# Strassen's algorithm in the second MLP layer of an attention and MLP kernel

## The chip, the cores and the metric

The kernel runs on one core of one Trainium2 chip. The metric is the device time of the whole kernel in microseconds (us).

## The reference

Attention inside routing clusters, then a layer norm and an MLP with a residual, all in float32:

```python
mask = q_assign[:, :, :, None] == k_assign[:, :, None, :]
scores = np.where(mask, scale * np.matmul(q, k.transpose(0, 1, 3, 2)), -1000000000.0)
attn = np.exp(scores - np.max(scores, axis=-1, keepdims=True))
attn = attn / (np.sum(attn, axis=-1, keepdims=True) + 1e-09)
x = np.matmul(attn, v)          # then (B, H, S, D) -> (B, S, H*D)
xn = (x - mu) / np.sqrt(var + 1e-06) * g_ln
out = x + np.maximum(xn @ w_ch1, 0.0) @ w_ch2
```

Four sequences (B) of 768 tokens (S), 8 heads of 64, model width 512 (DM), hidden width 2048 (FF).

## The kernel before

**Stages.** The attention part works through 16 pairs (a sequence and two heads), in an order of PE, DVE and ACT written out by hand. Beside it the float64 weights are loaded and turned into float32 (`w1`, `w2`), and the first sequence is normed. Each pair ends in `finish`: part 0 sums the denominators (`den_ps`, which ACT copies to `dsb`, sent by DMA to `rdens`), part 1 takes the reciprocal (L380) and spreads it through DRAM to `rb`, part 2 multiplies `x` by `rb` on DVE (L394) and stores it to DRAM (`xT_d`, L395). Then `stage.close()` gives the memory of the attention's pools back, the pools of the MLP (`ps_m`, `ps_o`, `ffn`, `ffn1`) are opened over it, and the MLP runs one sequence after the other. A new pool's first tile waits for whatever was last in the memory that the whole pool covers. In the MLP only PE's order is written by hand (`manual_schedule`); a scheduler sets the order of DVE, ACT and SP, which issues the DMAs.

**First layer.** `xn` holds a normed sequence, the 512 features on the partitions (4 chunks). Its product with `w1` is made by Strassen's algorithm on 2 x 2 blocks: seven products in place of eight, for each of 8 column tiles j (`first_layer`, parts 1 to 7; PE takes them as 1, 2, 4 of the tile before, 6, 3 of the tile before, 5, 7). One product is two matmuls of 384 columns. The block sums of the weights (`ws0` to `ws3`) are made once, by `weight_sum` on DVE in pairs 8 to 11; the sums of blocks of `xn` are made by `x_sum` (L472). Partial sums stay in PSUM (`x_ps`, `z_ps`) and are taken out by ACT (`kept`) and DVE (`add_relu`). The result is 32 tiles `hidden[r, f]` of 128 x 384 (r: half of the tokens, f: chunk of 128 hidden features).

**Second layer.** `project` takes the 6 token tiles t in turn: 16 matmuls of 512 columns (`hidden` is the stationary operand, `w2` the moving one) add up in a bank `o_ps` (L644), DVE adds the rows `xb` of the residual (L654), SP stores the sum. A float32 matmul is two MATMUL instructions, each with a weight load of its own, in the trace.

**The next sequence** is normed inside the second layer: `norm_load` after t = 0, `norm_rows` (12 transposes by PE, copies by ACT into two `xr` buffers in turn, which DMAs store and whose statistics DVE takes) after t = 1 and after t = 2, `norm_stat_rows` in the middle of t = 3 (PE transposes the statistics, DMAs spread them to `stat_row`), `norm_apply` (L449, L451) and `x_sum` after t = 4.

Of the kernel before, what the change touches and what calls it, by code (L numbers as in the profile page):

```python
# [8 lines left out]
F32 = mybir.dt.float32  # L9
# [10 lines left out]
def kernel(  # L20
# [35 lines left out]
    def pool(name, bufs, **kw):  # L56
        return stage.enter_context(tc.tile_pool(name=name, bufs=bufs, **kw))
# [12 lines left out]
    def ps(name, dt=F32, n=512):  # L70
        return pools["t"].tile([P, n], dt, tag="t", name=name)
# [35 lines left out]

    onehots = []
    for side in "qk":
        oh = const.tile([P, TH, NHALF, 2, D], BF16, name=f"onehot_{side}")  # L110
        nc.gpsimd.memset(oh, 0.0)
        onehots.append(oh)

# [42 lines left out]
    def w1_block(i, l, cols):  # L156
        return w1[:, l * NDH : (l + 1) * NDH, i * FH + cols.start : i * FH + cols.stop]

    def weight_sum(i, cols):

        a, op, b = (
            (w1_block(1, 0, cols), ALU.add, w1_block(1, 1, cols)),
            (ws[0][:, :, cols], ALU.subtract, w1_block(0, 0, cols)),
            (w1_block(0, 0, cols), ALU.subtract, w1_block(1, 0, cols)),
            (w1_block(0, 1, cols), ALU.subtract, ws[1][:, :, cols]),
        )[i]
        nc.vector.tensor_tensor(ws[i][:, :, cols], a, b, op)  # L167

# [289 lines left out]
    def x_sum(b, i):

        if i == 0:  # L460
            normed[b][1:] = [
                ffn.tile([P, NDH, HC], F32, tag=f"xt{m}", name=f"xt{m}", bufs=1)
                for m in range(3)
            ]
        _, t1, t2, t4 = normed[b]
        o, a, c = (
            (t1, x_block(b, 0, 1), x_block(b, 0, 0)),
            (t2, x_block(b, 1, 1), t1),
            (x_block(b, 0, 1), x_block(b, 1, 1), x_block(b, 0, 1)),
            (t4, x_block(b, 1, 0), t2),  # L470
        )[i]
        nc.vector.tensor_tensor(o, a, c, ALU.subtract)  # L472
# [4 lines left out]
    def put(n, slot, f, *args):  # L477
        extra.setdefault((n, slot), []).append(lambda: f(*args))
# [96 lines left out]
    def product(bank, lhs, rhs, cols, first):  # L575
        for c in range(NDH):
            nc.tensor.matmul(  # L577
                bank[:, :HC], lhs[:, c, cols], rhs[:, c, :],
                start=first and c == 0, stop=c == NDH - 1,
                skip_group_check=True,  # L580
            )

    def hidden_tile(r, f):
        h = (ffn, ffn1)[r].tile([P, HC], F32, tag=f"h{r}", name=f"h{r}", bufs=NFC + 1)
        hidden[r, f] = h
        return h

    def kept(bank, tag):
        t = ffn.tile([P, HC], F32, tag=tag, name=tag)
        nc.scalar.copy(t, bank[:, :HC])  # L590
        return t

# [5 lines left out]
    sets = {}  # L598

    def first_layer(b, j, part):  # L600

        _, t1, t2, t4 = normed[b]
        cols = slice(j * P, (j + 1) * P)
        every = slice(0, FH)
        st = sets.setdefault((b, j), {})
        if part == 1:
            st["x"] = ps_m.tile([P, 512], F32, tag="x", name="x_ps")
            product(st["x"], w1_block(0, 0, every), x_block(b, 0, 0), cols, True)  # L610
            st["p1"] = kept(st["x"], "p1")
        elif part == 2:
            y = ps_m.tile([P, 512], F32, tag="y", name="y_ps", bufs=1)
            product(y, w1_block(0, 1, every), x_block(b, 1, 0), cols, True)
            add_relu(0, j, y, st["p1"])
        elif part == 6:
            product(st["x"], ws[1], t2, cols, False)
            st["u2"] = kept(st["x"], "u2")
        elif part == 5:
            st["z"] = ps_m.tile([P, 512], F32, tag="z", name="z_ps")  # L620
            product(st["z"], ws[0], t1, cols, True)
        elif part == 7:
            product(st["x"], ws[2], x_block(b, 0, 1), cols, False)
            st["u3"] = kept(st["x"], "u3")
            add_relu(1, NFH + j, st["z"], st["u3"])
        elif part == 4:
            product(st["x"], w1_block(1, 1, every), t4, cols, False)
            nc.scalar.activation(hidden_tile(0, NFH + j), st["x"][:, :HC], AF.Relu)  # L628
        elif part == 3:
            product(st["z"], ws[3], x_block(b, 1, 1), cols, False)  # L630
            add_relu(1, j, st["z"], st["u2"])

    def rows_load(b, t):
        x = ffn1.tile([P, DM], F32, tag="xb", name="xb", bufs=3)
# [4 lines left out]
    chunks = [i * NFH + j for j in range(NFH) for i in range(2)]

    def project(b, t, x, fs, op):
        r, tt = divmod(t, TH)
        for f in fs:
# [7 lines left out]
        if fs[-1] != chunks[-1]:
            return
        o = ffn1.tile([P, DM], F32, tag="o", name="o_sb", bufs=2)
        nc.vector.tensor_tensor(o, op, x, ALU.add)  # L654
        nc.sync.dma_start(out=out[b].rearrange("(p c) m -> p c m", p=P)[:, t, :], in_=o)

    with tc.manual_schedule(engines={mybir.EngineType.PE}):
        for i in range(4):
            x_sum(0, i)
        for b in range(B):  # L660
            for j in range(NFH):
                for part, ahead in ((1, 0), (2, 0), (4, 1), (6, 0), (3, 1), (5, 0), (7, 0)):
                    if j - ahead >= 0:
                        first_layer(b, j - ahead, part)
            xb = {0: rows_load(b, 0)}
            for t in range(NT):
                if t + 1 < NT:
# [12 lines left out]
                if t == 0:  # L680
                    norm_load(b + 1)
                elif t < 3:
                    for tt in range(TH):
                        norm_rows(b + 1, (t - 1) * TH + tt)
                    if t == 2:
                        norm_stats(b + 1)
                elif t == 4:
# [206 lines left out]
```

## Time and profile before

| | |
|---|---|
| three runs, us | 1034.55, 1034.86, 1035.57 (median 1034.86) |
| the profiled execution's own time, us | 1035.45 |
| its span, us | 1033.6 |
| granted TensorE clock, mean | 0.994 |
| attention, from the start to the first MLP matmul | 394 us |
| MLP | 394 us to the end: four first layers, four second layers |
| busy in the second layer of the second sequence (626 to 714 us) | PE 88.0, DVE 21.3, ACT 4.8 us |

The time is the span plus about 2 us around it. Busy PE is the union of its matmuls, whose ends are modelled; how much time a stream of matmuls takes is read from the chain of waits, which has each stretch of equal matmuls with its length and their number. The second layers are the largest piece of the chain (32% of the span), the first layers 28%.

### The profile page before, as it was taken

What the parts mean: (1) busy time and instruction counts of PE and PEld (TensorE: products, weight loads), DVE (VectorE), ACT (ScalarE), POOL (GpSimd) and SP (SyncE); (2) the same over time, 40 slices, a digit from 0 to 9 for tenths busy, and PEclk for the clock granted to TensorE, in tenths of its full rate; (3) what the DMA queues carried; (4) which work ended last, traced back from release to release, by engine and by line L of the source; (5) the groups of instructions that cost most, each with busy time, mean ns of one, the idle gap of its engine ahead of it and who ended that gap; (6) DMA issues with size and microseconds to landing.
All of it is one profiled execution on the core that took longest, in us unless ns stands there. A gap on an engine that the chain in (4) does not pass through costs nothing.

```text
span 1033.6 us, 11347 instructions
## 1 busy us (share of the span) xinstructions
PE 1011.8 (98%) x4374; PEld 498.2 (48%) x4374; DVE 508.2 (49%) x860; ACT 314.9 (30%) x516; POOL 2.8 (0%) x27
## 2 busy tenths in 40 slices
PE   6999999999999998999999999999999999999997
PEld 3444444444444444554445554444555444555443
DVE  3888888999999995321241331151222151331000
ACT  4656666667565651220101220000220000221000
POOL 1000000000000000000000000000000000000000
PEclk8999999999999999999999999999999999999999
DMA  7355555555645322002221001231000331000100
GB/s 164 87 145 143 134 138 150 142 142 137 168 126 137 100 72 92 1 0 82 76 77 41 1 1 59 73 102 41 0 1 23 110 103 41 1 1 0 41 30 23
DMA packets 104765, 77.62 MB, mean 75 GB/s; under 512 B 84176, under 2 KB 84224, under 8 KB 104704
## 3 DMA queue, kind: packets, MB, share of 16 engines
q1 hardware_dynamic: 104032, 76.79, 26.4%
q8 instruction: 36, 0.59, 0.2%
q14 instruction: 25, 0.20, 0.1%
q10 hardware_dynamic: 672, 0.03, 0.0%
HBM read 57.71 MB, written 19.00 MB: 74 GB/s over the span
## 4 chain that ended last, share of the span: by engine, by line
PE 88%; DVE 9%; issue 1%; DMA 1%; ACT 0%; SPq 0%; DVEq 0%; ACTq 0%
PE o_ps L644 32%; PE x_ps L577 16%; PE a_ps L340 9%; PE s_ps L325 9%; PE z_ps L577 8%; PE y_ps L577 4%; PE s_ps L320 3%; DVE es L354 3%; PE qk_ps L231 2%; PE x_ps L413 1%; PE sim_ps L248 1%; PE oh_ps L296 1%; PE den_ps L371 1%; DVE es L351 1%; DVE ws L167 1%
## 5 line engine op out<-in xcount | busy, mean ns | idle before, releaser
L644 PE MATMUL o_ps<-w,h 128*128 128x512 f32 x768 | 332.2, 592 | 0.0
L644 PEld LDWEIGHTS o_ps<-w,h 128*128 128x128 f32 x768 | 145.2, 190 | 178.7 <-issue 176.6
L330 ACT ACTIVATE e<-s_ps 128x768 f32<-128x768 f32 x192 | 152.3, 814 | 71.8 <-PE s_ps L325 59.6
L325 PE MATMUL s_ps<-t,t 64*128 64x384 f32 x768 | 156.4, 486 | 0.0
L340 PE MATMUL a_ps<-e,v_sb 128*64 128x384 f32 x768 | 144.8, 499 | 0.0
L595 DVE TENSOR_TENSOR h<-z_ps,u 128x384 f32<-128x384 f32 x64 | 35.7, 558 | 205.6 <-PE z_ps L577 130.3
L354 DVE TENSOR_TENSOR es<-es,e 128x768 f32<-128x768 f32 x128 | 122.2, 954 | 7.3 <-ACT e L330 0.8
L654 DVE TENSOR_TENSOR o_sb<-o_ps,xb 128x512 f32<-128x512 f32 x24 | 16.6, 691 | 186.7 <-PE o_ps L644 186.7
L340 PEld LDWEIGHTS a_ps<-e,v_sb 128*64 128x64 f32 x768 | 46.6, 136 | 86.5 <-issue 86.3
L325 PEld LDWEIGHTS s_ps<-t,t 64*128 64x128 f32 x768 | 69.2, 190 | 21.4 <-issue 21.4
L590 ACT COPY u<-x_ps 128x384 f32<-128x384 f32 x64 | 30.7, 479 | 139.7 <-PE x_ps L577 139.7
L320 PE MATMUL s_ps<-m,m 64*128 64x384 bf16 x384 | 63.9, 330 | 0.6 <-ACT e L330 0.6
L590 ACT COPY p<-x_ps 128x384 f32<-128x384 f32 x32 | 15.3, 479 | 129.8 <-PE x_ps L577 129.8
L577 PE MATMUL z_ps<-xn,ws 128*128 128x384 f32 x128 | 46.8, 488 | 2.4 <-DVE h L595 2.4
L628 ACT ACTIVATE h<-x_ps 128x384 f32<-128x384 f32 x32 | 15.7, 491 | 108.8 <-PE x_ps L577 108.8
L577 PE MATMUL z_ps<-xt,ws 128*128 128x384 f32 x128 | 47.8, 497 | 0.0
L577 PE MATMUL x_ps<-xn,ws 128*128 128x384 f32 x128 | 46.8, 488 | 0.0
L577 PE MATMUL x_ps<-xn,w 128*128 128x384 f32 x128 | 46.6, 487 | 0.0
L577 PE MATMUL x_ps<-xt,ws 128*128 128x384 f32 x128 | 46.5, 486 | 0.0
L577 PE MATMUL y_ps<-xn,w 128*128 128x384 f32 x128 | 46.5, 486 | 0.0
L577 PE MATMUL x_ps<-xt,w 128*128 128x384 f32 x128 | 46.5, 486 | 0.0
L417 ACT COPY xr<-x_ps 128x512 f32<-128x512 f32 x24 | 13.5, 588 | 101.2 <-PE x_ps L413 86.4
(101 smaller groups left out, 798.0 us busy)
## 6 DMA issues: line engine op xcount, KB each, us to landing
raw<-in_moe_w_ch_dram SPq DMA_DIRECT2D x32, 512.0 KB, 3.9
q_sb<-in_q_dram SPq DMA_DIRECT2D x32, 192.0 KB, 4.3
k_sb<-in_k_dram SPq DMA_DIRECT2D x32, 192.0 KB, 4.3
v_sb<-in_v_dram SPq DMA_DIRECT2D x32, 192.0 KB, 4.1
rb<-row SPq DMA_DIRECT2D x32, 192.0 KB, 3.4
xT_d<-x SPq DMA_DIRECT2D x16, 384.0 KB, 3.0
xn<-xT_d SPq DMA_DIRECT2D x16, 384.0 KB, 4.6
x_d<-xr SPq DMA_DIRECT2D x24, 256.0 KB, 2.8
```

Of the source, the lines that this page charges most:

```text
L231: nc.tensor.transpose(t[:, c * P : (c + 1) * P], src[:, g * TH + c, :, :].rearrange("p h d -> p (h d)"), ident,)
L320: nc.tensor.matmul(s[:, j, :HC], st["m", 1][rows[j], keys], st["m", 0][rows[j], cols], start=True, stop=False,)
L325: nc.tensor.matmul(s[:, j, :HC], st[1][rows[j], keys], st[0][rows[j], cols], start=False, stop=True,)
L330: nc.scalar.activation(e, s[:, :, :HC], AF.Exp, scale=SCALE)
L340: nc.tensor.matmul(acc[j * D : (j + 1) * D, :HC], loaded[n]["v"][:, c, j, :], e[:, j, :], start=(c == 0), stop=(c == NT - 1),)
L354: nc.vector.tensor_tensor(es, es, soft.pop(i), ALU.add)
L577: nc.tensor.matmul(bank[:, :HC], lhs[:, c, cols], rhs[:, c, :], start=first and c == 0, stop=c == NDH - 1, skip_group_check=True,)
L590: nc.scalar.copy(t, bank[:, :HC])
L595: nc.vector.tensor_tensor(h, bank[:, :HC], other, ALU.add)
L628: nc.scalar.activation(hidden_tile(0, NFH + j), st["x"][:, :HC], AF.Relu)
L644: nc.tensor.matmul(op, hidden[r, f][:, tt * P : (tt + 1) * P], w2[:, f, :], start=(f == chunks[0]), stop=(f == chunks[-1]),)
L654: nc.vector.tensor_tensor(o, op, x, ALU.add)
```

## The change

The second layer is made by Strassen's algorithm too. Its blocks are halves of the tokens (r), of the hidden features (l) and of the 512 output columns (`MH` = 256): seven products in place of eight, each of 3 token tiles tt by 8 matmuls of 256 columns (`second_layer`, parts 1 to 7). One kind of product is taken over all tt before the next, in the order 1, 2, 5, 6, 7, 4, 3. The sums of blocks of `hidden` (`hidden_sums`) are made by DVE, three of the four in place; those of `w2` (`w2_sum`) and of `w1` (`w1_sums`) are made again in every sequence, so `weight_sum` goes from the attention part. `xb` is loaded in halves of 256 columns, and the output is added and stored in such halves. `ffn1` goes: all tiles of the MLP lie in one pool `ffn`; its PSUM tiles lie in one pool of 8 banks. `norm_rows` moves behind parts 2 and 5, `norm_stat_rows` behind the first tile of part 6, `norm_apply` behind part 7, `x_sums` behind part 4. The two `onehot` tiles move to a pool that ends with the attention.

```diff
-    ws = [weights.tile([P, NDH, FH], F32, name=f"ws{i}") for i in range(4)]
...
-    for i in range(4):
-        for o in range(2):
-            put(8 + 2 * o + i // 2, (0, 3)[i % 2], weight_sum, i, slice(o * WC, (o + 1) * WC))
...
-    ps_m = pool("ps_m", 2, space=PSUM)
-    pools["t"] = pool("ps_o", 3, space=PSUM)
+    pools["t"] = pool("ps_m", 8, space=PSUM)
     ffn = pool("ffn", 2)
-    ffn1 = pool("ffn1", 1)
...
+    def w1_sums(b, j):
+        t = ffn.tile([P, 4, NDH, P], F32, tag="ws", name="ws")
...
+            nc.vector.tensor_tensor(t[:, i], x, y, op)
...
+    def w2_sum(st, i):
+        if i in (1, 3):
+            st["t", i] = ffn.tile([P, NFH, MH], F32, tag="sums", name=f"w2t{i}")
+        elif i == 2:
+            st["t", 2] = ffn.tile([P, NFH, MH], F32, tag="sums", name="w2t2")
...
+        for c in range(0, NFH, 2):
+            nc.vector.tensor_tensor(o[:, c : c + 2], x[:, c : c + 2], y[:, c : c + 2], ALU.subtract)
+
+    def hidden_sums(c, late):
+
+        a11, a12, a21, a22 = [hidden[r, l, c] for r in range(2) for l in range(2)]
+        if late:
+            nc.vector.tensor_tensor(a12, a12, a11, ALU.subtract)
+            return
+        s3 = ffn.tile([P, HC], F32, tag="hs", name="hs", bufs=NFH)
...
+        nc.vector.tensor_tensor(s3, a11, a21, ALU.subtract)
+        nc.vector.tensor_tensor(a21, a21, a22, ALU.add)
+        nc.vector.tensor_tensor(a11, a21, a11, ALU.subtract)
+
+    def second_product(bank, tt, lhs, rhs, first):
+        for c in range(NFH):
             nc.tensor.matmul(
-                op,
-                hidden[r, f][:, tt * P : (tt + 1) * P],
-                w2[:, f, :],
...
+                bank[:, :MH], hidden[lhs + (c,)][:, tt * P : (tt + 1) * P], rhs[:, c, :],
...
+    def add_rows(b, r, tt, j, bank):
+
+        x = ffn.tile([P, MH], F32, tag="xb", name="xb", bufs=4)
+        nc.sync.dma_start(out=x, in_=x_d[b][:, r * TH + tt, j * MH : (j + 1) * MH])
+        o = ffn.tile([P, MH], F32, tag="o", name="o_sb", bufs=12)
+        nc.vector.tensor_tensor(o, bank[:, :MH], x, ALU.add)
+        return o
...
+    def second_layer(b, tt, part, st):
+        if part == 1:
+            st["x", tt] = ps("x_ps")
+            second_product(st["x", tt], tt, (0, 0), w2_block(0, 0), True)
+            st["p1", tt] = add_rows(b, 0, tt, 0, st["x", tt])
+        elif part == 2:
+            y = ps("y_ps")
+            second_product(y, tt, (0, 1), w2_block(1, 0), True)
+            add_store(b, 0, tt, 0, st["p1", tt], y)
+        elif part == 5:
+            st["z", tt] = ps("z_ps")
+            second_product(st["z", tt], tt, (1, 0), st["t", 1], True)
+        elif part == 6:
+            second_product(st["x", tt], tt, (0, 0), st["t", 2], False)
+            st["u2", tt] = add_rows(b, 0, tt, 1, st["x", tt])
+        elif part == 7:
+            second_product(st["x", tt], tt, ("s3",), st["t", 3], False)
+            st["u3", tt] = add_rows(b, 1, tt, 1, st["x", tt])
+            add_store(b, 1, tt, 1, st["u3", tt], st["z", tt])
+        elif part == 4:
+            second_product(st["x", tt], tt, (1, 1), st["t", 2], False)
+            store(b, 1, tt, 0, add_rows(b, 1, tt, 0, st["x", tt]))
+        elif part == 3:
+            second_product(st["z", tt], tt, (0, 1), w2_block(1, 1), False)
+            add_store(b, 0, tt, 1, st["u2", tt], st["z", tt])
...
+            for tt in range(TH):
+                second_layer(b, tt, 1, st)
+                if tt == 0:
+                    first_layer(b, NFH - 1, 4)
+                    first_layer(b, NFH - 1, 3)
+            for c in range(NFH):
+                hidden_sums(c, False)
+            w2_sum(st, 2)
+            if more:
+                norm_load(b + 1)
+            for part in (2, 5, 6, 7, 4, 3):
+                for tt in range(TH):
+                    second_layer(b, tt, part, st)
+                    if part == 6 and tt == 0 and more:
+                        norm_stat_rows(b + 1)
+                if part == 2:
+                    for c in range(NFH):
+                        hidden_sums(c, True)
+                if part == 5:
+                    w2_sum(st, 3)
+                if part == 6:
+                    w2_sum(st, 4)
+                if more and part in (2, 5):
...
+                        norm_rows(b + 1, (0 if part == 2 else TH) + tt)
+                    if part == 5:
+                        norm_stats(b + 1)
+                if more and part == 7:
...
+                            norm_apply(b + 1, i, c)
+                if more and part == 4:
+                    x_sums(b + 1)
```

Two places of the order that the scheduler makes of it. First DVE from attention to MLP, before: `x<-x,rb` (L394) is part 2 of `finish`, L380 and L554 to L558 are part 1 for the last pair and a check that follows it, `xt` and `xn<-xn` are the sums of `xn` (L472), of which three more stand ahead of these rows, `h` the first hidden tiles.

```order
L472 TENSOR_TENSOR xt_4062<-xn,xt_4061 128x768
L595 TENSOR_TENSOR h_4075<-y_ps,p_4070 128x384
L596 TENSOR_SCALAR h_4075<-h_4075 128x384
L380 RECIPROCAL rdens<-rdens 128x12
L554 TENSOR_REDUCE ends<-rdens 128x1
L555 TENSOR_REDUCE ends<-rdens 128x1
L556 TENSOR_SCALAR ends<-ends 128x1
L557 TENSOR_SCALAR ends<-ends 128x1
L558 TENSOR_TENSOR ends<-ends 128x1
L595 TENSOR_TENSOR h_4100<-y_ps,p_4095 128x384
L596 TENSOR_SCALAR h_4100<-h_4100 128x384
L394 TENSOR_TENSOR x<-x,rb 128x768
```

And with the change (L387 is L394 of before, L373 is L380, L456 to L461 are the sums of `xn`, `ws` those of `w1`):

```order
L387 TENSOR_TENSOR x<-x,rb 128x768
L373 RECIPROCAL rdens<-rdens 128x12
L540 TENSOR_REDUCE ends<-rdens 128x1
L541 TENSOR_REDUCE ends<-rdens 128x1
L542 TENSOR_SCALAR ends<-ends 128x1
L543 TENSOR_SCALAR ends<-ends 128x1
L544 TENSOR_TENSOR ends<-ends 128x1
L387 TENSOR_TENSOR x<-x,rb 128x768
L456 TENSOR_TENSOR xt<-xn 128x768
L578 TENSOR_TENSOR ws<-w_163 128x256
L457 TENSOR_TENSOR xt<-xn,xt 128x768
L458 TENSOR_TENSOR xn<-xn 128x2x384
```

The sums of `xn` stood ahead of the last pair's reciprocal and of its L394; now they stand behind both. In the program with the change the first of them, `xt<-xn`, waits for the DMA that stores the last pair's `x` (`xT_d<-x`), because the one pool `ffn` reaches over the memory of `x` and `rb`; `ffn` of before did not, `ffn1` did.

Second, DVE behind part 5 and the second group of `norm_rows`, with the change: BN_STATS and BN_AGGR are the statistics of its three rows, `w2t` sums of `w2`, `o_sb` the first tile of part 6, L421 and L422 end the statistics that PE then transposes, L442 is `norm_apply`.

```order
L643 TENSOR_TENSOR w2t_4547<-w_164 128x512 x4
L413 BN_STATS bn<-xr 128x6 x2
L414 BN_AGGR mv<-bn 128x2 x2
L413 BN_STATS bn<-xr 128x6
L414 BN_AGGR mv<-bn 128x2
L421 COPY stat<-mv 128x6
L670 TENSOR_TENSOR o_sb<-x_ps,xb 128x256
L422 RECIPROCAL stat<-stat 128x6
L670 TENSOR_TENSOR o_sb<-x_ps,xb 128x256
L643 TENSOR_TENSOR w2t_4435<-w_164,w2t_4435 128x512 x2
L442 TENSOR_TENSOR xn<-xn,stat_row 128x768
L643 TENSOR_TENSOR w2t_4435<-w_164,w2t_4435 128x512
```

Before, no sum stood ahead of the statistics (L428 and L429 are L421 and L422 here, L449 is L442):

```order
L654 TENSOR_TENSOR o_sb<-o_ps,xb 128x512
L420 BN_STATS bn<-xr 128x6 x2
L421 BN_AGGR mv<-bn 128x2 x2
L420 BN_STATS bn<-xr 128x6
L421 BN_AGGR mv<-bn 128x2
L428 COPY stat<-mv 128x6
L429 RECIPROCAL stat<-stat 128x6
L449 TENSOR_TENSOR xn<-xn,stat_row 128x768 x2
L654 TENSOR_TENSOR o_sb<-o_ps,xb 128x512
```

The sums `w2t<-w` of four instructions, which wait for the end of part 5, now stand ahead of the second group's statistics, and the first output tile of part 6 ahead of the reciprocal.

## Rows read from the trace of the kernel before

**Rows 1.** Page, part 4: shares of the chain that ended last
```profile
PE 88%; DVE 9%; issue 1%; DMA 1%; ACT 0%; SPq 0%; DVEq 0%; ACTq 0%
```

**Rows 2.** Chain of waits in order of time: start us, us, what
```profile
464.37 2.58 PE z_ps L577 x8
...
498.29 1.44 PE x_ps L413 x12
...
955.75 70.40 PE o_ps L644 x164
...
224.28 0.67 PE oh_ps L296 x12
```

**Rows 3.** Groups by line, shapes apart: busy us, mean ns | idle before us, releaser
```profile
L644 PEld LDWEIGHTS o_ps<-w,h 128*128 128x128 f32 x768 | 145.2, 190 | 178.7 <-issue 176.6
...
L219 DVE TENSOR_TENSOR w<-tb,ta 128x512 f32<-128x512 f32 x32 | 22.1, 691 | 1.1
...
L273 DVE TENSOR_TENSOR hit<-simT_ps,best 128x384 f32<-128x384 f32 x16 | 8.9, 557 | 0.6
...
L296 PEld LDWEIGHTS <-onehot_k 128*128 128x128 bf16 x96 | 6.3, 101 | 0.0
```

**Rows 4.** Chain of waits, last matmuls on `v` of a slot, four pair ends
```profile
27.07 1.44 PE a_ps L340 x8
...
50.33 1.44 PE a_ps L340 x8
...
215.45 1.44 PE a_ps L340 x8
...
333.57 1.44 PE a_ps L340 x8
```

**Rows 5.** Groups by line: the block sums of the weights
```profile
L167 DVE TENSOR_TENSOR ws<-w 128x1024 f32<-128x1024 f32 x4 | 4.8, 1210 | 0.0
```

**Rows 6.** Timeline, attention to MLP: start us, us, engine, instruction [idle before, releaser]
```profile
394.11 0.48 ACT L376 COPY dsb<-den_ps 128x384 f32<-128x384 f32 x1 [3.53 <-PE den_ps L371]
...
404.26 0.95 DVE L394 TENSOR_TENSOR x<-x,rb 128x768 f32<-128x768 f32 x1
...
405.23 0.33 SPq L395 DMA_DIRECT2D xT_d<-x  x1
...
407.62 0.56 DVE L595 TENSOR_TENSOR h<-z_ps,u 128x384 f32<-128x384 f32 x1 [2.41 <-DMA xT_d<-x]
...
408.23 1.70 PE L577 MATMUL z_ps<-xn,ws 128*128 128x384 f32 x4 [2.37 <-DVE h L595]
```

**Rows 7.** Stretches behind that stop: us, busy us (x) of five engines, PEclk, DMA share, GB/s
```profile
409.00:410.00 1.00, 1.00 (x4) 0.63 (x3) 0.03 (x1) 0.00 (x0) 0.00 (x0) 0.76 0.87 311
...
412.00:413.00 1.00, 1.00 (x3) 0.40 (x2) 0.00 (x0) 0.00 (x0) 0.00 (x0) 0.54 0.00 0
```

**Rows 8.** The same at the kernel's start
```profile
14.00:15.00 1.00, 0.38 (x4) 0.38 (x5) 0.80 (x3) 0.00 (x0) 0.00 (x0) 0.50 1.30 212
...
19.00:20.00 1.00, 1.00 (x8) 0.53 (x4) 0.00 (x0) 0.99 (x2) 0.00 (x0) 0.50 0.92 210
```

**Rows 9.** Timeline, statistics of the second sequence
```profile
513.30 1.60 PE L413 MATMUL x_ps<-ident,xn 128*128 128x128 f32 x12
...
514.56 1.29 DVE L420 BATCH_NORM_STATS2 bn<-xr 128x6 f32<-128x512 f32 x2 [0.37 <-ACT xr L417]
...
517.07 0.59 ACT L417 COPY xr<-x_ps 128x512 f32<-128x512 f32 x1 [2.06 <-DMA x_d<-xr]
...
519.30 0.19 DVE L429 RECIPROCAL stat<-stat 128x6 f32<-128x6 f32 x1 [0.50 <-ACT stat L427]
...
521.61 0.27 PE L434 MATMUL stat_ps<-ident,stat 128*12 128x128 f32 x1
...
527.39 1.83 DVE L449 TENSOR_TENSOR xn<-xn,stat_row 128x768 f32<-128x768 f32 x2 [7.90 <-DMA stat_row<-stat_d]
```

**Rows 10.** Second layer of the second sequence as one stretch, columns as in rows 7
```profile
626.00:714.00 88.00, 88.00 (x226) 40.50 (x225) 21.27 (x36) 4.82 (x10) 0.00 (x0) 1.00 0.22 75
```

More of the change, by code (lines that the diff above doesn't have):

```diff
@@ L109 @@
     for side in "qk":
-        oh = const.tile([P, TH, NHALF, 2, D], BF16, name=f"onehot_{side}")
+        oh = route.tile([P, TH, NHALF, 2, D], BF16, name=f"onehot_{side}")
         nc.gpsimd.memset(oh, 0.0)
@@ L153, with w1_block @@
     FH = FF // 2
-    ws = [weights.tile([P, NDH, FH], F32, name=f"ws{i}") for i in range(4)]
[L156 to L167, printed above, removed]
+    def w1_block(i, l, j):
+        return w1[:, l * NDH : (l + 1) * NDH, i * FH + j * P : i * FH + (j + 1) * P]
     WC = 512
@@ L456, in x_block, with x_sums @@
         return normed[b][0][:, l * NDH : (l + 1) * NDH, j * HC : (j + 1) * HC]
[L458 to L472, printed above, removed]
+    def x_sums(b):
+        t = ffn.tile([P, 3, NDH, HC], F32, tag="sums", name="xt")
+        normed[b][1:] = [t[:, m] for m in range(3)]
+        t1, t2, t4 = normed[b][1:]
+        nc.vector.tensor_tensor(t1, x_block(b, 0, 1), x_block(b, 0, 0), ALU.subtract)
+        nc.vector.tensor_tensor(t2, x_block(b, 1, 1), t1, ALU.subtract)
+        nc.vector.tensor_tensor(
+            x_block(b, 0, 1), x_block(b, 1, 1), x_block(b, 0, 1), ALU.subtract
+        )
+        nc.vector.tensor_tensor(t4, x_block(b, 1, 0), t2, ALU.subtract)
     extra = {}
@@ L581, in product, with kept @@
             )
+    def w1_sums(b, j):
+        t = ffn.tile([P, 4, NDH, P], F32, tag="ws", name="ws")
+        sets[b, j] = {"s": [t[:, i] for i in range(4)]}
+        for i, (x, op, y) in enumerate((
+            (w1_block(1, 0, j), ALU.add, w1_block(1, 1, j)),
+            (t[:, 0], ALU.subtract, w1_block(0, 0, j)),
+            (w1_block(0, 0, j), ALU.subtract, w1_block(1, 0, j)),
+            (w1_block(0, 1, j), ALU.subtract, t[:, 1]),
+        )):
+            nc.vector.tensor_tensor(t[:, i], x, y, op)
     def hidden_tile(r, f):
-        h = (ffn, ffn1)[r].tile([P, HC], F32, tag=f"h{r}", name=f"h{r}", bufs=NFC + 1)
-        hidden[r, f] = h
-        return h
-    def kept(bank, tag):
-        t = ffn.tile([P, HC], F32, tag=tag, name=tag)
+        l, c = divmod(f, NFH)
+        h = ffn.tile([P, HC], F32, tag=f"h{r}{l}", name=f"h{r}{l}", bufs=NFH)
+        hidden[r, l, c] = h
+        return h
+    def kept(bank, name):
+        t = ffn.tile([P, HC], F32, tag="p", name=name, bufs=5)
         nc.scalar.copy(t, bank[:, :HC])
@@ L639, with w2_block @@
[L639 to L643, printed above, removed]
-            nc.tensor.matmul(
-                op,
-                hidden[r, f][:, tt * P : (tt + 1) * P],
-                w2[:, f, :],
-                start=(f == chunks[0]),
-                stop=(f == chunks[-1]),
-            )
[L651 to L655, printed above, removed]
+    def w2_block(l, j):
+        return w2[:, l * NFH : (l + 1) * NFH, j * MH : (j + 1) * MH]
@@ new lines, in hidden_sums @@
+    def hidden_sums(c, late):
[4 more added lines that the diff above has]
+        s3 = ffn.tile([P, HC], F32, tag="hs", name="hs", bufs=NFH)
+        hidden["s3", c] = s3
+        nc.vector.tensor_tensor(s3, a11, a21, ALU.subtract)
[3 more added lines that the diff above has]
+        for c in range(NFH):
+            nc.tensor.matmul(
+                bank[:, :MH], hidden[lhs + (c,)][:, tt * P : (tt + 1) * P], rhs[:, c, :],
+                start=first and c == 0, stop=c == NFH - 1,
+                skip_group_check=True,
+            )
@@ new lines, in add_rows, with store @@
+    def add_rows(b, r, tt, j, bank):
[4 more added lines that the diff above has]
+        return o
+    def store(b, r, tt, j, o):
+        nc.sync.dma_start(
+            out=out[b].rearrange("(p c) m -> p c m", p=P)[
+                :, r * TH + tt, j * MH : (j + 1) * MH
+            ],
+            in_=o,
+        )
@@ new lines, in add_store @@
+    def add_store(b, r, tt, j, o, bank):
+        nc.vector.tensor_tensor(o, bank[:, :MH], o, ALU.add)
+        store(b, r, tt, j, o)
+    def second_layer(b, tt, part, st):
[4 more added lines that the diff above has]
+        elif part == 2:
+            y = ps("y_ps")
+            second_product(y, tt, (0, 1), w2_block(1, 0), True)
[16 more added lines that the diff above has]
+            add_store(b, 0, tt, 1, st["u2", tt], st["z", tt])
@@ L657 @@
     with tc.manual_schedule(engines={mybir.EngineType.PE}):
-        for i in range(4):
-            x_sum(0, i)
+        x_sums(0)
         for b in range(B):
+            st = {}
+            w1_sums(b, 0)
             for j in range(NFH):
+                if j + 1 < NFH:
+                    w1_sums(b, j + 1)
                 for part, ahead in ((1, 0), (2, 0), (4, 1), (6, 0), (3, 1), (5, 0), (7, 0)):
```

65 lines of the change are left out of this document (24 added, 41 removed).

## The prediction

> **What bounds the kernel now.** I read the shares of the chain of waits first: PE holds 88% of it [rows 1], so a change counts by what it takes from PE's stream or puts as a gap into it. The chain in order of time gives the prices. In the last second layer 164 MATMULs of 512 columns take 70.40 us [rows 2], 429.3 ns each; in a first layer 8 of 384 columns take 2.58 us, 322.5 ns each. Both are columns / 1.2 per ns (426.7 and 320 ns) plus some 2.5 ns: PE streams without gaps, and DVE is busy for 21.3 of 88 us there [rows 10]. Then I read the timeline where this stream breaks: at the seam from attention to MLP [rows 6], and where the next sequence's statistics are due [rows 9].
>
> **Step 1, second layer on PE.** Before: 4 sequences x 6 x 16 x 2 = 768 MATMULs [rows 3] x 429.3 ns = 329.7 us. Now: 4 x 7 x 3 x 8 x 2 = 1344 MATMULs of 256 columns. No row has this size; 256 / 1.2 = 213.3 ns plus an overhead. Its low end is the 2.5 ns above. Its high end is the stream of 128-column transposes, 12 in 1.44 us [rows 2]: 120 ns each, 13.3 over 106.7. What could add more is the weight load, 190 ns each [rows 3]: it hides under 427 or 320 ns of streaming, and has 23 ns to spare under 213.3. Loads also overlap one another: those of `oh_ps` last 101 ns each [rows 3], yet 12 such matmuls pass in 0.67 us [rows 2], 56 ns apart. So I take the low end, nearest in kind (float32, two instructions): 215.8 ns x 1344 = 290.0 us. **Gain 39.7 us**; at the high end (226.7 ns) 25.0 us.
>
> The Trainium skill, page "TensorE: Matmul & The Clock Gate", section "Back-to-back issue gap", speaks against small matmuls: in a stream of pairs both weight load and matmul set the spacing, 81 ns at 128 columns where the matmul's formula alone gives 55.8. The `oh_ps` row, 56 ns at 128 columns, disagrees with the 81 ns.
>
> **Step 2, the seam.** Now the sums of `xn` wait for the store of the last pair's `x` (first place of the order). That store is issued at 405.23 us, and what waited for it before, an `h` tile, went at 407.62 [rows 6]; nothing ahead of it changes. From there DVE runs, to the second sum of `w1` that part 6 needs: four sums of 768 (0.95 each, as L394, [rows 6]) and two of 256 columns. No row has 256; 512 columns take 691 and 384 take 557 ns [rows 3], and on that line 256 take 0.42 (0.557 at the most). 407.62 + 4 x 0.95 + 2 x 0.42 = 412.3 us. PE meanwhile has only parts 1 and 2 of the first tile: it starts them when ACT has copied `dsb` at 394.6 [rows 6] and is through 2.6 us later, at 397.2. It stands 15.1 us. From 412.3, 52 of the first layer's 54 products remain at 1.29 us [rows 2]: 67.1 us, to 479.4. Before, three products from 464.37 on, at 1.29 us each [rows 2], brought PE to the second layer at 468.24, with a stop of 2.4 us behind it [rows 6]. The clock adds to it: 1.5 us behind the short stop it fell to its lower level, 1.2 GHz, until shortly before 413 us [rows 7] (first and last of four stretches), which cost 1.7 us; at the kernel's start it was low when PE came back at 14.6 us, and still low beyond 19 us [rows 8], which cost about 3. After 15 us of standing I take the middle, 2.4. Second layer at 481.8: **loss 13.6 us**. Ends: 11.2 with no slow clock, 17 if the low clock lasts as at the start and some backlog of DVE shows.
>
> **Step 3, the statistics.** In three sequences PE transposes the statistics inside the second layer. Before, the second group of row transposes began at 513.30, the statistics were ready 6.2 us later (519.30 + 0.19), and PE got there 8.3 us later, at 521.61 [rows 9]: 2.1 us to spare. Now PE gets there after 12 transposes (1.44), a wait of some 0.25 for a bank (the third row's takes that of the first, whose copy must be over), and one tile of part 6 (16 x 0.2158 = 3.45): 5.1 us. DVE has four sums of 512 columns (4 x 0.69, [rows 3]) ahead of the statistics, from the end of part 5 on: to 2.9; then the statistics of two rows (1.29 and their two short ends, [rows 9]), to 4.5. The third row's copy ends at 4.4, held by the DMA of the first as before (517.07 + 0.59); from there to the end of the reciprocal took 1.8 us (to 519.49). So they are ready at 4.5 + 1.8 = 6.3, PE waits 1.2 us, and with the bank 1.45 are lost. **Loss 3 x 1.45 = 4.4 us**; ends 0, and 3 x 3 = 9 if each wait brings the low clock as at [rows 7].
>
> **Step 4, attention.** 8 sums of 1.2 us [rows 5] leave DVE. A pair takes 23.26 us where only PE counts (27.07 to 50.33); the five pairs from 215.45 to 333.57, where the sums stood, take 118.1 [rows 4], 1.8 more than 5 x 23.26. Of it 0.6 are PE's own transposes. **Gain 1.2 us**, ends 0 and 1.8.
>
> **What costs nothing, and what hides it.** DVE gets per sequence 32 sums of 256 (0.42), 32 of 384 (0.557), 16 of 512 (0.69) and 18 output halves for 6 whole ones: 46 us. It has 67 us free in a second layer of 88 [rows 10] and more in the first layer; half of the sums stand in either. If this cover were gone the 46 us would lie on PE's path. In the order, the tightest places are behind L442, which waits for `stat_row`, 5.8 us after the transposition S (521.61 to 527.39, [rows 9]). Behind it on DVE are the last sums of `w2` for part 4 (done at S + 8.6, due at S + 17.4) and the output tile that frees the bank of part 7's third tile (S + 10.1, due at S + 13.9). The block sums of `hidden` have a part of 10.4 us ahead of their use. `norm_load` is issued as soon as `xn` is free, 17 us ahead of the first transposes. SP's loads of `xb` wait only for tiles given back four uses earlier. The last output is half as wide: 0.3 us gained at the end.
>
> **Sum**, against the profiled execution, 1035.45 us (0.6 above the median of the three runs, which is within 0.06%): 1035.45 - 39.7 - 1.2 - 0.3 + 13.6 + 4.4 = 1012.3, so **1012 us**. With all ends: 1004 (11.2, 0, 1.8) to 1022 (17, 9, 0).
>
> **Rivals.**
> 1. Weight loads show by as much as in the transposes (13.3 ns). For: that row; against: those are other, single-pass matmuls, with other moving data. 1344 x 10.9 ns = 14.6 us more: 1027. Chance 0.07.
> 2. The loads set the spacing, and the kernel is slower. For: 190 of 213 ns; pairs of 384-column matmuls of `a_ps` share the array, and 8 take 1.44 us [rows 4], so a pair 360 ns, 40 over 320. Against: `oh_ps`. At 40 ns, 1344 x 37.5 ns = 50 us more: 1062. It decides from 17 ns over 215.8, where the gain of 23.2 is eaten. Chance 0.05. (The rule of the Trainium skill's page in step 1 points this way: its difference of 25 ns on 1344 matmuls would be 34 us, by an estimate from the page 1046 us; the trace's 56 ns does not agree.)
> 3. No stop at the seam: the change does what it says and no wait holds the sums back (only PE's early parts are late). Against: the wait stands in the program. 1012 - 13.6 = 998 us; chance 0.05.
> 4. DVE's order holds PE up in each second layer, from L442 on: if `stat_row` comes over 3.8 us later than before, each later us costs PE one. For: SP has more DMAs (256-column halves). 2 us in three sequences, and the same again in clock: 1022; chance 0.07.
>
> My forecast has 0.76. Rivals 1, 2 and 3 lie outside 1004 to 1022: 0.17, so the range holds about 0.8. About 0.2% (2 us) is what can be told from no change; faster by more: 0.94, slower: 0.05, same: 0.01.
>
> **What would show it.** Right: 16 MATMULs of the second layer in 3.45 us of the chain; PE idle from about 397 to 412 us, released by a sum of `w1` or `xn`; a wait of PE of about 1 us for L422 three times; no other wait of PE above 0.3 us in the MLP. Wrong: a spacing above 220 ns (step 1), PE going on at 397 us (step 2), or PE waiting for `h`, `w2t` or `o_sb` at the change of a part (the cover).

## The result and the profile after

The changed kernel takes 1007.36 us (median of 4 runs, 1006.54 to 1008.26), the kernel before 1034.70 (4 runs, 1034.48 to 1035.57): ratio 0.9734, 95% interval 0.9718 to 0.9751. The prediction was 1012, range 1004 to 1022. The profiled execution of the changed kernel took 1008.26 us, its span 1006.5.

The shares of the chain (page, part 4), in answer to [rows 1]: PE rose from 88% to 96%.

```profile
PE 96%; DMA 1%; DVE 1%; SPq 0%; ACT 0%; issue 0%; DVEq 0%
```

The longer stretches of the chain in order of time (start us, us, what), in answer to [rows 2]: the first three rows lie at the seam, the others in the second layer of the first sequence.

```profile
408.27 2.90 PE x_ps L563 x4
411.17 2.21 PE z_ps L563 x4
413.38 2.58 PE x_ps L563 x8
...
477.88 3.45 PE x_ps L659 x16
...
483.91 6.91 PE x_ps L659 x32
490.82 10.36 PE y_ps L659 x48
...
502.49 10.36 PE z_ps L659 x48
...
514.62 3.47 PE x_ps L659 x16
...
518.96 27.63 PE x_ps L659 x128
546.59 10.36 PE z_ps L659 x48
```

Three things are to be seen. 48 MATMULs of 256 columns take 10.36 us, 215.8 ns each. The stream of the layer is broken for the last two products of the first layer (481.33 to 483.91), for the first group of row transposes (501.18 to 502.49), and twice with a wait in it. The second group of row transposes takes from 502.49 + 10.36 = 512.85 to 514.62, 1.77 us; 12 transposes took 1.44 before, so 0.33 are lost. The statistics take from 514.62 + 3.47 = 518.09 to 518.96, 0.87 us, where the same place of the chain before has 0.10 (521.78 to 521.88); so 0.76 are lost. And from this second layer to the next one (626.61 in the same view) a sequence takes 148.73 us.

What PE waited for, by line (us in total, times, longest us). Of waits before the MLP the rows are left out:

```profile
PE x_ps L563 <- DVE ws L578: 14.5, 1, 14.5
...
PE stat_ps L427 <- DVE stat L422: 1.8, 3, 0.6
PE x_ps L406 <- ACT xr L410: 0.7, 3, 0.2
PE x_ps L563 <- ACT dsb L369: 0.6, 1, 0.6
```

The same view of the kernel before has two other waits there, and neither is in the list above:

```profile
PE den_ps L371 <- DVE es L354: 2.4, 1, 2.4
PE z_ps L577 <- DVE h L595: 2.4, 1, 2.4
```

The seam in the timeline (start us, us, engine, instruction, in brackets the idle time before it and its releaser), in answer to [rows 6]:

```profile
388.70 1.63 PE L364 MATMUL den_ps<-es,ones 128*32 128x384 f32 x8
...
390.93 1.56 PE L563 MATMUL x_ps<-xn,w 128*128 128x384 f32 x4 [0.59 <-ACT dsb L369]
392.32 1.45 PE L563 MATMUL y_ps<-xn,w 128*128 128x384 f32 x4
...
401.52 0.33 SPq L388 DMA_DIRECT2D xT_d<-x  x1
...
403.94 0.96 DVE L456 TENSOR_TENSOR xt<-xn 128x768 f32<-128x768 f32 x1 [2.45 <-DMA xT_d<-x]
403.99 0.48 ACT L589 COPY p<-x_ps 128x384 f32<-128x384 f32 x1 [13.12 <-DMA xT_d<-x]
...
407.76 0.42 DVE L578 TENSOR_TENSOR ws<-ws,w 128x256 f32<-128x256 f32 x1
...
408.27 2.90 PE L563 MATMUL x_ps<-xt,ws 128*128 128x384 f32 x4 [14.50 <-DVE ws L578]
```

PE makes two products, then stands for 14.5 us until the second sum `ws`. The chain of waits behind that sum runs back over the store of the last pair's `x` (2.30 us from its issue), the product L387 at 400.53 and three DMAs one after the other (`rdens`, `row`, `rb`) to the copy `dsb` at 390.39. A second tile of the pool waits for the same store: ACT's copy `p` of the first product, which part 6 needs as well, since it adds to the bank that `p` is taken from. It is done 3.7 us ahead of the sum, so the sum decides. The clock in this stretch, in answer to [rows 7] (busy us of five engines, granted clock, DMA share, GB/s):

```profile
391.00:395.00 4.00, 2.77 (x8) 1.36 (x8) 0.30 (x2) 0.00 (x0) 0.00 (x0) 1.00 0.28 100
395.00:400.00 5.00, 0.00 (x0) 0.00 (x0) 0.89 (x5) 0.00 (x0) 0.00 (x0) 0.58 0.31 80
...
411.00:412.00 1.00, 1.00 (x3) 0.64 (x2) 1.00 (x2) 0.48 (x1) 0.00 (x0) 0.50 0.00 0
412.00:413.00 1.00, 1.00 (x3) 0.45 (x2) 1.00 (x3) 0.00 (x0) 0.00 (x0) 0.56 0.00 0
413.00:414.00 1.00, 1.00 (x5) 0.60 (x4) 0.32 (x1) 0.00 (x0) 0.00 (x0) 1.00 0.00 0
```

The clock fell to its lower level while PE stood and came back shortly before 413 us, over 4 us after PE went on. The two products made meanwhile took 2.90 and 2.21 us in place of 1.29 each: 2.5 us lost. This loss differs from run to run, with such a stop (13.1 to 16.0 us) ahead of it: by the chain it is 1.6 us in e2, 1.7 in e6, 1.8 in e3, 2.6 in e4, 2.9 in e5 and 3.2 in e7. A difference of 1 or 2 us between two kernels that both have the stop can therefore not be read from their times alone; the length of a sequence in the chain, which lies behind the seam, tells more.

The statistics of the second sequence, in answer to [rows 9]:

```profile
512.69 1.04 PE L406 MATMUL x_ps<-ident,xn 128*128 128x128 f32 x8
512.89 2.50 DVE L643 TENSOR_TENSOR w2t<-w 128x512 f32<-128x512 f32 x4 [6.82 <-PE z_ps L659]
...
515.30 1.28 DVE L413 BATCH_NORM_STATS2 bn<-xr 128x6 f32<-128x512 f32 x2
516.09 0.58 ACT L410 COPY xr<-x_ps 128x512 f32<-128x512 f32 x1 [1.69 <-DVE bn L413]
...
518.45 0.18 DVE L422 RECIPROCAL stat<-stat 128x6 f32<-128x6 f32 x1
...
518.69 0.28 PE L427 MATMUL stat_ps<-ident,stat 128*12 128x128 f32 x1 [0.61 <-DVE stat L422]
```

### The profile page after: what moved, and what is told of

It is laid out like the page before. It is cut to its first block, busy times and chain, and to the rows that moved or that the text cites. A ratio compares the mean times of both kernels' runs of the same rounds, so it can differ in the third digit from the quotient of the medians.

```text
span 1006.5 us, 13062 instructions
## 1 busy us (share of the span) xinstructions
PE 972.9 (97%) x4950; PEld 607.7 (60%) x4950; DVE 657.3 (65%) x1232; ACT 314.7 (31%) x516; POOL 2.8 (0%) x27
## 4 chain that ended last, share of the span: by engine, by line
PE 96%; DMA 1%; DVE 1%; SPq 0%; ACT 0%; issue 0%; DVEq 0%
PE x_ps L659 16%; PE x_ps L563 16%; PE a_ps L333 14%; PE s_ps L318 12%; PE z_ps L563 8%; PE z_ps L659 8%; PE s_ps L313 4%; PE y_ps L659 4%; PE y_ps L563 4%; PE qk_ps L224 3%; PE sim_ps L241 1%; PE oh_ps L289 1%; PE den_ps L364 1%; PE x_ps L406 1%; PE simT_ps L257 1%; DMA k_sb<-in_k_dram 0%
## 5 line engine op out<-in xcount | busy, mean ns | idle before, releaser
L659 PE MATMUL x_ps<-w2t,h 128*128 128x256 f32 x384 | 84.7, 379 | 0.0
L659 PEld LDWEIGHTS x_ps<-w2t,h 128*128 128x128 f32 x384 | 72.5, 190 | 9.6
L578 DVE TENSOR_TENSOR ws<-w 128x256 f32<-128x256 f32 x64 | 24.8, 420 | 68.0 <-PE z_ps L563 68.0
L563 PE MATMUL x_ps<-xt,ws 128*128 128x384 f32 x128 | 47.9, 498 | 14.5 <-DVE ws L578 14.5
L670 DVE TENSOR_TENSOR o_sb<-x_ps,xb 128x256 f32<-128x256 f32 x48 | 20.2, 420 | 59.7 <-PE x_ps L659 59.6
L563 PE MATMUL z_ps<-xt,ws 128*128 128x384 f32 x128 | 47.5, 494 | 0.0
L563 PE MATMUL x_ps<-xn,w 128*128 128x384 f32 x128 | 46.6, 487 | 0.6 <-ACT dsb L369 0.6
L563 PE MATMUL x_ps<-xt,w 128*128 128x384 f32 x128 | 46.5, 486 | 0.0
L563 PE MATMUL z_ps<-xn,ws 128*128 128x384 f32 x128 | 46.5, 486 | 0.0
L563 PE MATMUL y_ps<-xn,w 128*128 128x384 f32 x128 | 46.5, 486 | 0.0
L563 PE MATMUL x_ps<-xn,ws 128*128 128x384 f32 x128 | 46.5, 486 | 0.0
L313 PEld LDWEIGHTS <-m 64*128 64x128 bf16 x384 | 18.6, 93 | 44.1 <-issue 29.0
```

What stands on the lines that cost most here:

```text
L313: nc.tensor.matmul(s[:, j, :HC], st["m", 1][rows[j], keys], st["m", 0][rows[j], cols], start=True, stop=False,)
L563: nc.tensor.matmul(bank[:, :HC], lhs[:, c, :], rhs[:, c, :], start=first and c == 0, stop=c == NDH - 1, skip_group_check=True,)
L578: nc.vector.tensor_tensor(t[:, i], x, y, op)
L659: nc.tensor.matmul(bank[:, :MH], hidden[lhs + (c,)][:, tt * P : (tt + 1) * P], rhs[:, c, :], start=first and c == 0, stop=c == NFH - 1, sk ...
L670: nc.vector.tensor_tensor(o, bank[:, :MH], x, ALU.add)
```

## The experiments

Each kernel was timed beside the kernel before, e1 to e4 in one series (before: 1034.78 us), e5 to e8 in a second (1034.87 us). The ratio is to the kernel before.

| run | edit to the changed kernel | us | ratio, 95% interval |
|---|---|---|---|
| e1_seam | pool of the MLP split in two | 991.04 | 0.9575 (0.9562 to 0.9588) |
| e2_old_sums | eight sums of weights back in the attention | 1010.35 | 0.9765 (0.9751 to 0.9778) |
| e3_stat_late | statistics transposed one tile later | 1004.45 | 0.9708 (0.9695 to 0.9721) |
| e4_sum_order | third sum of `w2` behind the statistics | 1006.65 | 0.9728 (0.9714 to 0.9741) |
| e5_double_sums | most sums made twice | 1007.58 | 0.9731 (0.9716 to 0.9746) |
| e6_cols128 | second layer in matmuls of 128 columns | 1017.0 | 0.9828 (0.9813 to 0.9843) |
| e7_eight | second layer by eight plain products | 1044.88 | 1.0092 (1.0076 to 1.0107) |
| e8_seam_late | e1 and e3 together | 988.11 | 0.9548 (0.9535 to 0.9561) |

### e1_seam: no store in the way

```diff
     ffn = pool("ffn", 2)
+    ffn1 = pool("ffn1", 2)
...
-        h = ffn.tile([P, HC], F32, tag=f"h{r}{l}", ...
+        h = (ffn if r == l else ffn1).tile([P, HC], F32, tag=f"h{r}{l}", ...
```

`hs`, `xb` and `o_sb` go to `ffn1` as well.

> The pool ffn is split: the sums, ws, p, h00 and h11 in a first pool that ends below the pool of x, rb and es, the rest in a second one behind it. Theory 1 (the stop at the seam is the wait of the sums of xn for the store of the last pair's x, and the low clock behind it): PE goes on behind its second product at about 393.5 us, 54 products of 1.29 us from 390.9 on bring it to the second layer at 460.6 in place of 477.9, so 17 us less: 990.3 us, and no granted clock below 1.0 between 391 and 470 us. Rival (the sums are late for another reason, DVE's order or the weights of that stage): PE still stands over 5 us at part 6 of the first tile, 995 us or more. Rival (the wait goes to the h10 tile, which now waits for the same store, as h did before the change): a stop of 2 to 3 us about ten products later, with a low clock behind it, 994 us.

991.04 us, 16.3 less than the change. The stop is gone and nothing of its size took its place (timeline of e1, where L564 is L563 of the change and L579 its L578):

```profile
389.85 1.56 PE L564 MATMUL x_ps<-xn,w 128*128 128x384 f32 x4 [0.59 <-ACT dsb L369]
391.24 1.45 PE L564 MATMUL y_ps<-xn,w 128*128 128x384 f32 x4
...
392.95 0.42 DVE L579 TENSOR_TENSOR ws<-ws,w 128x256 f32<-128x256 f32 x1
...
393.47 1.53 PE L564 MATMUL x_ps<-xt,ws 128*128 128x384 f32 x4 [0.78 <-issue]
```

Of the stop 0.78 us is left; the row names no releaser, but the second sum `ws` on DVE ends at 393.37 in this trace, 0.1 us ahead. The second layer starts at 460.79, 70.94 us behind the first product (86.95 in the change), which is the 16.0 us. The granted clock is 1.00 in every stretch from 391 to 480 us. The first tile of the second pool to be written is not `h10` but `h01`, by ACT for part 4 (L623), 2.48 us behind the issue of the store at 402.11; the first row that waited for the store in the change went 2.42 behind it. The first loads of `xb`, also of that pool, are issued at 404.49.

```profile
404.59 0.49 ACT L623 ACTIVATE h<-x_ps 128x384 f32<-128x384 f32 x1 [1.34 <-DVE ws L579]
```

The row names a sum `ws` as releaser, which that tile does not read; that it waits for the store is inferred from the times. PE shows no wait there. Theory 1 holds, both rivals fall. With the split the scheduler also puts the sums of `xn` ahead of the last pair's reciprocal again (389.14 and 394.29 in the trace), so e1 shows what the pool's place costs, the wait and the order that follows from it together; and as the sums, `ws` and `p` moved together, it does not price the three one by one. Stop and clock of the seam are thus worth 16 us in the changed kernel; before, the smaller stop cost 2.4 us, and its clock 2.0 by the chain, where two stretches of eight took 4.26 and 2.86 us in place of 2.58 each:

```profile
408.23 4.26 PE z_ps L577 x8
412.50 2.86 PE x_ps L577 x8
```

### e2_old_sums: what the attention gave

```diff
+            put(8 + 2 * o + i // 2, (0, 3)[i % 2], old_sum, i, slice(o * WC, (o + 1) * WC))
```

`old_sum` is the `weight_sum` of before with one tile in the pool `last` as its output.

> Eight sums of 1024 columns stand again on DVE in pairs 8 to 11, where weight_sum stood; nothing reads them. Theory 1 (their removal gave 1.3 us in the pairs and 2.4 us at the last denominators, where DVE came late, less 0.6 us of a new wait for dsb): 3.1 us slower than the change, 1010.4 us; den_ps waits for es by 2.4 us and the first MLP matmul starts at 394.0 in place of 390.9. Rival (as predicted, 1.2 us, and DVE's lag at the end of the attention has another source, such as onehots in another pool): 1008.6 us, no wait at den_ps.

1010.35 us, 3.0 more. The wait of before is back, with its size (PE's waits by line):

```profile
PE den_ps L364 <- DVE es L347: 2.4, 1, 2.4
```

The first MLP matmul starts at 393.99, as expected, and the stop at the seam ends 3.3 us later than in the change (411.60 in place of 408.27):

```profile
393.99 2.93 PE L580 MATMUL x_ps<-xn,w 128*128 128x384 f32 x4 [0.59 <-ACT dsb L369]
396.72 1.78 PE L580 MATMUL y_ps<-xn,w 128*128 128x384 f32 x4
...
411.60 2.90 PE L580 MATMUL x_ps<-xt,ws 128*128 128x384 f32 x4 [13.10 <-DVE ws L595]
```

The stop reads 13.1 in place of 14.5 us only because the two products ahead of it ran at the lower clock (0.50 from 394 to 396 us), which costs nothing here, since PE stands behind them anyway. In the kernel before, the same wait of 2.4 us left the clock at 1.00. Theory 1 holds. DVE's work of pairs 8 to 11 was not only a matter of the pairs that it stood in: DVE was then late to the end, and the last pair's denominators waited for it. In the kernel before, DVE was busy for 54.8 of the 57 us from 333 to 390, which leaves it little room to catch up.

### e3_stat_late and e4_sum_order: who holds the statistics

```diff
-                    if part == 6 and tt == 0 and more:
+                    if part == 6 and tt == 1 and more:
                         norm_stat_rows(b + 1)
```

> norm_stat_rows one token tile of part 6 later. Theory 1 (PE loses the time by which the statistics are later than one tile of part 6): the three waits of 0.6 us, 0.76 us by the chain, go: 2.3 us less than the change, 1005.1 us, and nothing in their place, since the tail behind L442 has 3.8 us to spare and is moved by 2.7. Rival (the tail decides: the sums and output tiles queued behind L442 on DVE hold PE up in part 7 or 4): PE waits there by 1 us or more three times, 1007 to 1010 us.

1004.45 us, 2.9 less. No wait for `stat` is left among PE's waits, and nothing in the MLP came in its place. The chain has the starts of two second layers:

```profile
476.20 3.45 PE x_ps L659 x16
...
624.15 3.45 PE x_ps L659 x16
```

A sequence takes 147.95 us in place of 148.73, 0.78 less, 2.3 in three sequences: theory 1 holds to its number. The other 0.6 us of the 2.9 are not the statistics'; from trace to trace the seam alone differs by as much (here the stop ends 0.95 us earlier than in the change, and its clock costs 0.7 less). e4 is the change with the statistics where they were, and another order on DVE:

```diff
-                if part == 5:
-                    w2_sum(st, 3)
...
                     if part == 5:
                         norm_stats(b + 1)
+                if part == 5:
+                    w2_sum(st, 3)
```

> The third sum of w2 is asked for behind the second group of row statistics in place of ahead of it; on DVE two of its four instructions then stand ahead of them, two among them. Theory 1 (the prediction's account: the sums and the third row's copy end almost together, 4.5 and 4.4 us behind the end of part 5): the wait of PE shrinks by 0.1 us at most per sequence, 1007.1 us. Rival (the four sums alone hold the statistics up, the third copy waits for DVE's statistics of the first row and not for its DMA): the wait shrinks by half or more, 1006.0 us or less.

1006.65 us, 0.7 less, with an interval of the ratio that overlaps that of the change; the times alone don't tell. The trace does. Waits of PE for the statistics (0.6 us, three times) are as in the change, a sequence takes 148.74 us (477.99 to 626.73) where it took 148.73, and the timeline of e4 is the same from the third row shown on:

```profile
512.80 1.04 PE L406 MATMUL x_ps<-ident,xn 128*128 128x128 f32 x8
...
514.21 1.28 DVE L413 BATCH_NORM_STATS2 bn<-xr 128x6 f32<-128x512 f32 x2
...
516.19 0.59 ACT L410 COPY xr<-x_ps 128x512 f32<-128x512 f32 x1 [1.67 <-DMA x_d<-xr]
516.79 1.28 ACT L420 ACT_TABLE_LOAD   x1
...
518.57 0.18 DVE L422 RECIPROCAL stat<-stat 128x6 f32<-128x6 f32 x1
```

The first row's statistics come 1.1 us earlier (514.21 against 515.30, with PE's transposes 0.11 later), but the third copy starts 3.39 us behind the first transposes as it did (3.40), released by the store of the first row and no longer by DVE. So theory 1 holds: two chains end together there, the sums and the store of a row, and taking the sums away frees nothing. The table load between the copy and the square root of the statistics (1.28 us on ACT) is part of the time from the copy's end to the reciprocal's, 1.96 us in the change; no run takes it out.

### e5_double_sums: how thick the cover is

```diff
-            nc.vector.tensor_tensor(t[:, i], x, y, op)
+            for _ in range(2):
+                nc.vector.tensor_tensor(t[:, i], x, y, op)
```

The same for `w2_sum` 1 and 2 and for `hs`.

> Every sum of w1, the first two sums of w2 and the sums hs are made twice in a row: 48 more DVE instructions per sequence, about 23 us, 93 us in all. Theory 1 (the sums lie beside PE's stream, and only those of the seam show): one more sum of w1 of 0.4 us twice in the stop at the seam, 1008.2 us, and no new wait of PE in the MLP over 1 us. Rival (DVE's cover is nearly used up): waits of PE for h, hs or w2t, and several tens of us of the 93, 1030 us or more.

1007.58 us, 0.2 more than the change, less than the spread of either. PE's only changed wait is the stop at the seam, 16.0 in place of 14.5 us, so 1.5 more where 0.8 was expected:

```profile
PE x_ps L563 <- DVE ws L579: 16.0, 1, 16.0
```

A sequence takes 148.74 us (479.42 to 628.16), as in the change. DVE is busy for 67.6 us more in the MLP (383.5 in place of 315.9 from 390 to 1005 us; the 93 expected are whole durations, and sums of one stream overlap), and behind the seam this costs nothing: theory 1 holds.

### e6_cols128: where weight loads begin to count

```diff
+            for w in range(0, MH, P):
                 nc.tensor.matmul(
-                    bank[:, :MH], ..., rhs[:, c, :],
+                    bank[:, w : w + P], ..., rhs[:, c, w : w + P],
```

Both halves of a product open the accumulation in their bank, so the sums of the second layer differ; only its time is read.

> Each matmul of the second layer is split into two of 128 columns, so 2688 MATMULs of 128 columns with as many weight loads. Theory 1 (the loads hide at any size, the overhead is 2.5 ns): 109.2 ns each, 293.5 us for the layers in place of 290.0, so 1010.9 us. Rival a (as the float32 transposes, 120 ns each): 322.6 us, 1040 us. Rival b (a load of 190 ns must be over before the next one starts, and had 26 ns to spare at 215.8 ns): 510.7 us, 1228 us.

1017.0 us, 9.6 more, between theory 1 and rival a. First the chain, then the groups by line (busy us, mean ns | idle before):

```profile
489.21 10.72 PE y_ps L660 x96
```

```profile
L660 PEld LDWEIGHTS x_ps<-w2t,h 128*128 128x128 f32 x768 | 86.6, 192 | 0.0
```

96 MATMULs in 10.72 us are 111.7 ns each, 5.0 over columns / 1.2; at 256 columns it was 2.5. 2688 x 111.7 = 300.2 us, 10.2 over the change. A sequence takes 151.25 us (475.91 to 627.16), 2.52 more, which is 10.1 us in four. Loads of 192 ns pass every 111.7 ns, so they overlap one another, and rival b falls by 200 us. Theory 1's size was off: the overhead is not the same at every width. Whether the load makes the 2.5 ns more is not shown.

### e7_eight: the number of products alone

```diff
+    def whole_product(b, tt, r, j, end=False):
+        bank = ps("x_ps")
+        second_product(bank, tt, (r, 0), w2_block(0, j), True)
...
+        second_product(bank, tt, (r, 1), w2_block(1, j), False)
+        store(b, r, tt, j, add_rows(b, r, tt, j, bank))
```

> The second layer by eight plain products of 256 columns in place of Strassen's seven, no sums of hidden or w2, everything else as in the change (statistics one product later). Theory 1 (the gain is the number of products alone, halving the columns costs nothing much): 1536 MATMULs x 215.8 ns = 331.5 us, 41.4 more than the change, less 2.3 for the waits at the statistics: 1046.5 us, so about 12 us slower than the kernel before (the seam, less the attention's gain). Rival (part of the gain comes from the new order of the second layer or from the banks): under 1040 us.

1044.88 us: 37.5 more than the change and 0.9% slower than the kernel before (by the ratio). A sequence takes 157.86 us (in the chain, the starts of two second layers):

```profile
636.21 3.45 PE x_ps L659 x16
...
794.07 3.45 PE x_ps L659 x16
```

That is 9.13 more than the change. 48 more matmuls are 10.36 us; the other way go the gaps at the statistics, 1.1 us by the chain above (0.33 + 0.76). 3 x 9.13 + 10.36 = 37.8 us; the times show 37.5. Theory 1 holds, with 3.3 in place of 2.3 us for the statistics.

### e8_seam_late: the best version

The two edits above together, the split pool and `tt == 1`:

```diff
+    ffn1 = pool("ffn1", 2)
...
-                    if part == 6 and tt == 0 and more:
+                    if part == 6 and tt == 1 and more:
```

> The split pools and the later statistics together. Theory 1 (the two losses are apart from one another and add): 991.0 less 2.9 (what the later statistics alone gave) = 988.1 us, PE without a wait over 0.8 us from 393 us on. Rival (with the seam closed DVE's work moves, and the statistics or the tail behind L442 take some back): 989.5 to 991 us.

988.11 us, 4.5% less than the kernel before and 1.9% less than the change. No wait for `stat` and no stop at the seam is left among PE's waits in the MLP; the longest is 0.8 us. A sequence takes 147.95 us (460.73 to 608.68) as in e3, 0.79 less than in e1 (148.74), so the two losses are apart from one another, and theory 1 holds. That the medians add to 0.1 us is luck in part: of the 2.9 us between e1 and e8 the chain shows 2.4 (3 x 0.79).

## Why the prediction was right

Against the profiled executions, 1035.45 and 1008.26 us, the terms were (gain minus, loss plus):

| step | predicted | measured | where |
|---|---|---|---|
| 1, PE in the second layer | -39.7 | -39.7 | 215.8 ns in the chain; e7 |
| 2, the seam | +13.6 | +13.3 | the timeline; e1 |
| 3, the statistics | +4.4 | +3.3 | the two gaps of the chain; e3, e4 |
| 4, attention | -1.2 | -3.7 | starts of `den_ps`, its wait; e2 |
| the end | -0.3 | -0.15 | last product to the end of the span |
| sum | 1012.3 | 1008.5 | measured: 1008.26 |

**Step 1** was right to the tenth of a nanosecond, and for its reason: 256 columns stream like 384 and 512. e7 shows that nothing else in the new layer gains. Rivals 1 and 2 (weight loads that show, by 10.9 or by over 17 ns) are ruled out at 256 columns, and in e6 even matmuls of 128 columns, with a load of 192 ns each, have only 2.5 ns more of overhead. The Trainium skill (page "TensorE: Matmul & The Clock Gate", section "Back-to-back issue gap") gives about 81 ns for a stream of pairs of 128 columns, 25 over the matmul's own formula. An overhead of that size is not borne out by e6, where float32 matmuls of 128 columns stand 5.0 ns over columns / 1.2.

**Step 2** was right in mechanism, in place and nearly in size: a stop of 14.5 us (15.1 predicted), 2.5 of clock (2.4). That the clock came out so close is luck: the 2.4 was the middle of two guesses, one of them low (1.7 behind the short stop of before, where the chain has 2.0), and in the runs with this stop the clock cost anything from 1.6 to 3.2. By the prediction's own account, which counts from the `dsb` copy, the loss is 86.95 - 74.26 = 12.7 between the first product and the second layer (before: 393.98 to 468.24), and 0.6 of the wait for `dsb`, 13.3. What was too long are the sums on DVE, by 0.4 us from the start of the first to the end of the second `ws` (4.2 in place of 4.6 us): those of one stream start every 0.87 and 0.34 us (405.15, 406.02; 408.09, 408.43 in the trace), not after their own 0.95 and 0.42. Rival 3, no stop, fell; e1 shows that it was a matter of one pool's place in memory, and not of Strassen's algorithm. The prediction named only the sums; the copy `p` waited for the store too.

**Step 3** was right in mechanism, and a third too high: 0.76 + 0.33 us per sequence in place of 1.45. The statistics were ready 5.94 us behind the first transposes (518.63 - 512.69), not 6.3, and PE got there after 5.40, not 5.1. The prediction saw both chains, the sums and the held copy, 0.1 us apart, and e4 confirms that the copy alone would do; the sums alone were not tried. The low clock did not come behind these waits: the 16 MATMULs behind the first took 3.47 us, and the 128 behind the second 27.63, 215.9 ns each. Rival 4, the tail behind L442, did not show, and e3, which moves it by 2.7 us, did not wake it.

**Step 4** is the term that was mis-sized, 1.2 us predicted and 3.7 measured, and a part of its mechanism was missing. The prediction took the gain from five pairs in the middle, 1.2 us beyond PE's own work; PE did come 1.29 us earlier to the last `den_ps` (388.70 in place of 389.99). But it left out that the eight sums were also the cause of DVE's lateness at the very end: the wait of 2.4 us at `den_ps` was in the trace of before, behind the last row of the stretch that was read, and it went. e2 shows the wait, and 3.0 us in all, after the 0.6 that the new wait for `dsb` takes back. How the 3.7 divide is less sure: the last `den_ps` starts at 389.33 in e2 and 389.99 before, and between 387.56 and 388.81 in the eight traces without the eight sums.

**The cover** held, with much to spare (e5). The misses of steps 2, 3 and 4 all lie on the same side, so none hides another. The forecast, 1012.3 before rounding, was 4.9 us above the median: 2.5 of it from step 4, 1.1 from step 3, 0.3 from step 2, 0.15 less from the end; 0.9 because the profiled execution of the changed kernel stands that much above its median, and 0.2 that no term accounts for. The kernel before was counted from its profiled execution too, which stands 0.75 above its median.

## What to carry to other kernels

Price a matmul by its stream: where the granted clock is full and no wait lies in it, float32 matmuls of 256, 384 and 512 columns cost their columns and 2.5 ns, so an algorithm with fewer products gains in proportion. Then look for the place where the new tiles take over old memory: one pool that reached over a tile with a store in flight gave back 16 us of the gain, and a split of the pool recovered them without touching the algorithm. An engine's lateness is paid where its result is next waited for, which may be several stages on: follow it to the end of the stage, and do not price its work only in the stretch where it stands.

## What the runs showed of the hardware

- The overhead of a float32 matmul with its own weight load is 2.5 ns at 256, 384 and 512 columns, 5.0 at 128 (e6). Transposes of 128 columns, 120 ns apart, are slower than matmuls of the same size, 111.7.
- Weight loads of 192 ns each follow one another every 111.7 ns (e6): 768 of them take 86.6 us, so they overlap.
- After the stop of 14.5 us the granted clock was at its lower level (0.50) for over 4 us while PE worked, and then 1.00 in the next stretch; over the seven traces with such a stop this cost 1.6 to 3.2 us. Behind the waits of 0.6 us it did not fall. Behind a wait of 2.4 us for the last pair's denominators it fell in e2 and not in the kernel before.
